# A phase's two pairs of attention scores in four neighbouring banks, with one exponential of 2048 columns

## The chip, the cores and the metric

The kernel runs on one core of a Trainium2 chip. The metric is the time of one execution in microseconds (us) of device time. All times below are in us unless they are marked ns. The engines go by the profile's names: PE is TensorE (its weight loads are PEld), ACT is ScalarE, DVE is VectorE, POOL is GpSimd and SP is SyncE, which issues the DMAs.

## The reference

The input x has 2048 tokens of 512 channels, in float32. Two branches are mixed by a gate of each token:

```python
g = sigmoid((x * gate_w).sum(-1, keepdims=True))
a = attention(x, wqkv, wo)       # 32 heads of 16, softmax over all 2048 keys
b = token_mlp(x, w1, b1, w2, b2) # layernorm, then gelu MLP 2048 -> 1792 -> 2048 over tokens
return g * a + (1 - g) * b

def attention(x, wqkv, wo):
    q, k, v = ...                # (1, 32, 2048, 16) each, from x @ wqkv
    scores = q @ k.T * 16 ** -0.5
    p = softmax(scores, axis=-1)
    return (p @ v).reshape(B, S, 512) @ wo
```

The attention has 32 heads of 2048 x 2048 scores, each of which goes through one exponential.

## The kernel before, in words

The first stages make v, the stacks of q and k, the layernorm and the first layer of the MLP. They fill about the first 278 us. The rest is the attention, and beside it PE does the second layer of the MLP, the late queries and the first half of the output projection.

**Phases.** The attention is a loop of 128 phases (L992). A group `grp` is a pair of heads over half of the queries; it has four phases (`PHASES`, `ph`), and there are 32 groups. A phase makes 16 tiles of scores, called units `n` = 0 to 15, each of 128 keys by 512 queries in one PSUM bank (matmul L1065). A matmul of scores uses 64 of PE's rows. For the first `n_b` units another matmul, from the list `beside`, runs in the other 64 rows (L1074). `n_b` is 14 in phases with a step of the second layer (16 tiles, three steps each, two phases a step) and 12 in phases with a late query or a projection. The order of the units is `in_turn`: 0 to 13, then 14 and 15, or 0 to 13, then 15 and 14.

**Who takes a score out of its bank.** Units in `SINGLE` (0, 2, 4, 6, 7, 8) go through one exponential of 512 columns on ACT (L1091). Units in `EVAC` (1, 3, 5, 9, 14, 15) are copied by DVE to SBUF (L1087), and one exponential of 3072 columns works on all six there (L1100). Units 10 and 11, and 12 and 13 (`TWO`), lie in two neighbouring banks each, as one tile `t`, and each pair goes through one exponential of 1024 columns (`exps`, L1029).

**Banks.** Seven of eight banks serve scores, the eighth (`dn`) the matmuls beside. `shares(n)` gives the order in which a phase uses the seven: unit n < 7 goes to bank `share[n]`, unit 7 to 9 to `share[n - 7]`. Then a second set of tiles is laid over the same banks: units 10 to 13 go to `share[3]` to `share[6]`, unit 14 to `share[0]`, unit 15 to `share[2]`, and `av`, in which the products with v add up, to `share[1]`. Both sets come from pools that are opened with `reuse_waits="tile"` (`regions`). The argument of `shares` is the bank that the phase before gives back last (`spare`).

**Products with v.** After its scores a phase multiplies exponentials with v (`apply_v`, L961, 64 matmuls a phase): first the three `HELD` pairs of the phase before, then this phase's five `TURNS`, of which (10, 11) and (12, 13) come last. DVE then adds `av` to the group's sum (L983). In a group's first phase the held pairs close the group before in `av`, and the new group starts in another bank, `twos[spare]`.

**The order is written out.** Inside `tc.manual_schedule` every engine works in the order of the program. `call(p, ...)` puts an action ahead of phase p's scores, DMAs on SP's queue above all; `on_dve(p, ...)` puts a step on DVE behind the copies of phase p, ahead of the additions from `av`; `amid` puts one between the copies. `fetch` issues the DMAs of a block of attention outputs and leaves three steps on DVE for later phases (`ats`): the product with the inverse sums, a rounded copy, and the rest. `fetch_right` and `fetch_o` fetch such blocks; `load_wq` brings rows of the last weights, with two steps on DVE; `end_constants` makes four small constants. In this late stage `p0` is 112.

Of the kernel before, what the change touches and what calls it, by code (L numbers as in the profile page):

```python
# [9 lines left out]
F32 = mybir.dt.float32  # L10
# [3 lines left out]
AF = mybir.ActivationFunctionType  # L14
ALU = mybir.AluOpType
AX = mybir.AxisListType
SYNC = mybir.DependencyInfo(mybir.DependencyClass.Sync, mybir.DependencyReason.DATA)
AHEAD_OF_USE = "the next group's scores find their stacks awaited"
REASON = "the two halves of the rows add to one bank"
EARLY = "a later instruction of this engine then waits for one engine alone"  # L20
# [3 lines left out]
P = 128  # L24
# [8 lines left out]
NB = 512  # L33
NQ = S // NB
VC = DH + 1
SCALE = DH**-0.5
# [24 lines left out]
def gated_mix(ctx: ExitStack, tc: tile.TileContext, a_x, a_wqkv, a_wo, b_w1, b_b1, b_w2, b_b2, gate_w, out):  # L61
    nc = tc.nc
# [115 lines left out]
    with tc.tile_pool(name="vp", bufs=1, side="right") as pool:  # L178
# [143 lines left out]
        y, t, w = (pool.tile([P, NS], F32, name=n) for n in "ytw")  # L322
# [103 lines left out]
    with tc.tile_pool(name="gl", bufs=2, side="right") as gl:  # L426
# [74 lines left out]
        for f0, cs in order.items():  # L501
            n = min(NB, F - f0) // P
# [32 lines left out]
    ptp = att_ctx.enter_context(tc.tile_pool(name="pt", bufs=2, reuse_waits="tile"))  # L535
# [10 lines left out]
    for i, p in reversed(list(enumerate(ps))):  # L546
        u = out_pool.tile([P, D], F32, name="row", bufs=3)
        at = NF - len(ps) + i
# [32 lines left out]
    PHASES, NSC, BANKS = 4, 16, 7  # L581
# [20 lines left out]
    wq, between = [], {}  # L602
# [84 lines left out]
    def call(at, *what):  # L687
        calls.setdefault(at, []).append(what)

    def on_dve(at, *what):  # L690
        later.setdefault(at, []).append(what)
# [42 lines left out]
    def load_wq(at):  # L734
        wq.extend(v_block(0)[:, 8 * n : 8 * n + 8].rearrange("p (i t) x -> p i t x", i=2) for n in range(2))
        raw = end.tile([P, QW], F32, name="o_sum", bufs=3).rearrange("p (i c) -> p i c", i=2)
        nc.gpsimd.memset(raw, 0.0)
        for j in range(4):
            nc.sync.dma_start(
                raw[32 * j : 32 * j + DH], a_wo[(H - 2) * DH : H * DH, :].rearrange("(i r) c -> r i c", i=2)  # L740
            )
        raw = raw.rearrange("p i (t x) -> p i t x", x=P)
        on_dve(at + 2, nc.vector.tensor_copy, wq[0], raw)
        on_dve(at + 3, nc.vector.tensor_tensor, wq[1], raw, wq[0].bitcast(F32), ALU.subtract)

    def invert(half, k, pairs, at):

# [128 lines left out]
    at, queries = 0, [(b, n) for n in (2, 3) for b in range(ND)]  # L876
    for t in range(NS):
        at = put(second_layer(t), at, [14] * 3)
        if queries:
            b, n = queries.pop(0)  # L880
            at = put_whole(late_query(b, n), at)
# [9 lines left out]
    for half in range(2):  # L891
        for k in range(ND):
            pairs = 3 if half and k == ND - 1 else 4
            p0 = PHASES * (half * NP + 4 * k + pairs) + 1
            call(p0, invert, half, k, pairs, p0 + (2, 2, 1, 0)[k] if half else p0 + 2)
    left, right = slice(0, NB), slice(NB, QW)
    for k in range(ND):
        p0 = PHASES * (NP + 4 * (k // 2 + 1)) + 3 + 4 * (k % 2)
        assert p0 + 3 < 2 * at
        call(p0, fetch_left, k, p0 + 2, p0 + 3, p0 + 3)  # L900
    p0 = 2 * at
    call(p0, open_end)
    on_dve(p0 + 13, end_constants)
    for k in range(ND):
        call(p0 + k, fetch_right, k, p0 + k + 2, p0 + k + 2, p0 + k + 2)
    for t in range(NH):
        at = put_whole(project(t), at)
        call(p0 + 2 * t, load_base, NH + t)
    assert p0 + 7 < 2 * (at - 4) and at == NG * PHASES // 2
    call(p0 + 4, fetch_o, 0, p0 + 6, p0 + 6, p0 + 7)  # L910
    call(p0 + 6, fetch_o, 1, p0 + 8, p0 + 8, p0 + 10)
    call(p0 + 7, load_wq, p0 + 7)
    call(p0 + 9, fetch_o, 2, p0 + 11, p0 + 12, p0 + 12)
    call(LAST, lambda: fetch_o(3, LAST, LAST, LAST, pairs=3))

    token, mark = (out_pool.tile([1, 1], F32, name=name, bufs=1) for name in ("token", "mark"))
# [3 lines left out]
    TWO = (10, 11), (12, 13)  # L920
    TURNS = [(0, 2), (4, 6), (7, 8), *TWO]
    HELD = [(1, 3), (5, 9), (14, 15)]

    def shares(n):

        for one in range(0, BANKS, 2):
            lows = [k for k in range(one)][::2] + [k for k in range(one + 1, BANKS)][::2]
            for third in lows:
                if n in (third, third + 1):
                    first, second = (low for low in lows if low != third)  # L930
                    return [first, first + 1, one, second, second + 1, 2 * third + 1 - n, n]


    def regions():
# [53 lines left out]
    with tc.manual_schedule(engines=engines):  # L988
# [3 lines left out]
        for p in range(LAST + 1):  # L992
            grp, ph = divmod(p, PHASES)
            second = ph % 2
# [28 lines left out]
                    turn = 1 - turn  # L1023

            def exps(n):
                pt = ptp.tile([P, 2, NB], F32, name="p2", bufs=len(TWO))
                where = [share[(j - BANKS) % BANKS] for j in (n - 1, n)]
                low = min(where)
                pairs_done.append(nc.scalar.activation(pt, twos[low, low + 1], AF.Exp, scale=SCALE))  # L1029
                for j, k in zip((n - 1, n), where):  # L1030
                    units[j] = *units[j][:3], pt[:, k - low, :]

            pairs_done = []
# [6 lines left out]
            for n in in_turn:  # L1040
                i, qb = head[n], qbs[n]
                c = at[i][qb]
                at[i][qb] += 1
                if n < TWO[0][0]:
                    if n >= BANKS:
                        ones[share[n - BANKS]] = psum.tile([P, NB], F32, name=f"s{share[n - BANKS]}")
                    s = ones[share[n % BANKS]]
                else:
                    if n == TWO[0][0]:
                        pool.__exit__(None, None, None)  # L1050
                        pool = regions()
                        psum = pool.__enter__()
                        twos = {}
                        for low in range(BANKS):
                            if low == share[1]:
                                av = psum.tile([P, NB], F32, name="av")
                            elif low in (share[0], share[2]):
                                twos[low] = psum.tile([P, NB], F32, name=f"u{low}")
                            elif low not in twos:
                                two = psum.tile([P, 2, NB], F32, name=f"t{low}")  # L1060
                                twos[low], twos[low + 1] = two[:, 0, :], two[:, 1, :]
                                twos[low, low + 1] = two
                    s = twos[share[2 if n == NSC - 1 else (n - BANKS) % BANKS]]
                rows_i = slice(i * HALF, i * HALF + ROWS)
                nc.tensor.matmul(  # L1065
                    s,
                    kt[grp][rows_i, c * P : (c + 1) * P],
                    qt[grp][rows_i, qb * NB : (qb + 1) * NB],
                    start=True,
                    stop=True,  # L1070
                )
                if n < n_b:
                    ps, a, b, begin, last, done = beside[n]
                    mm = nc.tensor.matmul(ps, a[half], b[half], start=begin and not second, stop=last and bool(second))  # L1074
                    if n == 0 and fence is not None:
                        tc.add_manual_dep(mm.ins, fence.ins.name, SYNC, reason=REASON)
                    if n == n_b - 1:
                        fence = nc.gpsimd.memset(token, 0.0)  # L1078
                        tc.add_manual_dep(fence.ins, mm.ins.name, SYNC, reason=REASON)
                if n == in_turn[-2]:  # L1080
                    if n_b and second and beside[-1][-1] in between:
                        between[beside[-1][-1]]()
                    for what, *args in amid.get(p, ()):
                        what(*args)
                if n in EVAC:
                    pt = evac[:, EVAC.index(n), :]
                    nc.vector.tensor_copy(pt, s)  # L1087
                    units[n] = i, c, qb, pt
                elif n in SINGLE:
                    pt = ptp.tile([P, NB], F32, name="p1", bufs=len(SINGLE))  # L1090
                    one = nc.scalar.activation(pt, s, AF.Exp, scale=SCALE)  # L1091
                    if n == SINGLE[-1] and p:
                        tc.add_manual_dep(one.ins, earlier.ins.name, SYNC, reason=EARLY)
                    units[n] = i, c, qb, pt
                else:
                    units[n] = i, c, qb, None
                    if n in (TWO[0][1], TWO[1][1]):
                        exps(n)
            for x in ([evac] if p < LAST else [evac[:, :2, :], evac[:, 2:, :]]):
                done = nc.scalar.activation(x, x, AF.Exp, scale=SCALE)  # L1100
            tc.add_manual_dep(done.ins, pairs_done[0].ins.name, SYNC, reason=EARLY)
            evac_done.append(done)
            earlier = pairs_done[1]
            if n_b and second and beside[-1][-1]:
                beside[-1][-1]()
            if p == 0:
# [14 lines left out]
            if ph == 0:  # L1121
                if held:
                    apply_v(av, grp - 1, held, final=True)
                    spare = share[3]
                    av = twos[spare]
                apply_v(av, grp, turns)
            elif p < LAST:
                apply_v(av, grp, held + turns, await_loads=ph == PHASES - 1)
            else:
                ot = sums[grp]  # L1130
                nc.vector.tensor_scalar_max(ot, ot, least[0])
                apply_v(av, grp, held + turns + now_held, final=True)
                last_ot = ot
# [170 lines left out]
```

## Time and profile before

| | us |
|---|---|
| median of 3 runs | 1266.68 |
| lowest and highest | 1266.62, 1266.8 |
| the profiled execution's own time | 1266.69 |
| its span in the profile | 1264.9 |
| granted clock of TensorE, mean | 0.999 |

The page shares the span out by engine, follows back the chain of work that ended last, and groups instructions by line, engine and tiles: a row has the count, the summed busy time, the mean length of one in ns, and the idle time before them with what ended it. The timeline lists instructions in order of time: start, length, engine, line, operation, tiles, shape and count, where neighbours that are alike are put together; in brackets stands idle time of the engine just before, with what ended it. A start on ACT may lie before the end of the instruction ahead of it, so lengths there overlap.

### The profile page before, as it was taken

To read this page: it belongs to the slowest core of one execution; us is meant where nothing else is said; L and a number is where in the kernel's file an instruction comes from. 1 tells how busy PE (TensorE), PEld (TensorE's weight loads), DVE (VectorE), ACT (ScalarE), POOL (GpSimd) and SP (SyncE) were. 2 spreads that over 40 slices of the span, in tenths; PEclk is the share of its full clock that TensorE was granted. 3 is DMA by queue.
4 is the path that set the end of the run, shared out by engine and by line. 5 is a ranking of instruction groups with operands and counts; after the bars stand their busy time and mean duration, and the time that the engine had idled before them with its cause. 6 is when DMAs were issued, how large, how long until landed. Compare 5 with 4: busy or idle time off the path is not lost.

```text
span 1264.9 us, 32830 instructions
## 1 busy us (share of the span) xinstructions
PE 1255.3 (99%) x13342; PEld 828.8 (66%) x13342; DVE 857.4 (68%) x1562; ACT 1069.2 (85%) x1405; POOL 198.9 (16%) x316
## 2 busy tenths in 40 slices
PE   9999999999999999999999999999999999999997
PEld 7888888875666666666666666666666666666656
DVE  5675453178767676767677677777777677678883
ACT  4443343269999999999999999999999999999980
POOL 0220444461010101010110101111111111100000
PEclk9999999999999999999999999999999999999999
DMA  4799443244744544634344433444553443366611
GB/s 134 255 327 339 140 123 105 80 128 114 210 123 102 92 99 83 160 83 97 84 101 95 106 85 79 93 90 80 113 101 81 80 99 60 56 166 185 143 58 70
DMA packets 100556, 152.32 MB, mean 120 GB/s; under 512 B 17109, under 2 KB 56171, under 8 KB 96300
## 3 DMA queue, kind: packets, MB, share of 16 engines
q1 hardware_dynamic: 99820, 149.08, 46.3%
q8 instruction: 107, 1.75, 0.6%
q10 hardware_dynamic: 576, 1.05, 0.2%
q14 instruction: 53, 0.43, 0.1%
HBM read 105.39 MB, written 44.68 MB: 119 GB/s over the span
## 4 chain that ended last, share of the span: by engine, by line
PE 95%; DVE 2%; ACT 2%; DMA 0%; issue 0%; SPq 0%; DVEq 0%; ACTq 0%
PE av L961 30%; PE s L1065 20%; PE acc L424 12%; PE acc L75 8%; PE t L1065 8%; PE t L961 5%; PE dn L1074 4%; PE u L1065 3%; PE pa L1156 2%; DVE pe L1087 2%; ACT pe L1100 1%; ACT p L1091 1%; PE acc L199 1%; PE acc L268 1%; ACT p L1029 0%; DVE ot L983 0%
## 5 line engine op out<-in xcount | busy, mean ns | idle before, releaser
L1091 ACT ACTIVATE p<-s 128x512 f32<-128x512 f32 x768 | 412.2, 786 | 0.1
L1100 ACT ACTIVATE pe<-pe 128x3072 f32<-128x3072 f32 x129 | 380.6, 2952 | 0.6 <-DVE pe L1087 0.6
L1065 PE MATMUL s<-qs,ks 64*128 64x512 f32 x1280 | 330.6, 400 | 0.8 <-ACT p L1091 0.6
L1087 DVE COPY pe<-s 128x512 f32<-128x512 f32 x512 | 323.9, 686 | 5.5 <-PE s L1065 1.7
L1065 PEld LDWEIGHTS s<-qs,ks 64*128 64x128 f32 x1280 | 225.6, 184 | 94.3 <-issue 52.3
L1029 ACT ACTIVATE p<-t 128x1024 f32<-128x1024 f32 x256 | 277.6, 1259 | 0.0
L961 PE MATMUL av<-p,v 128*32 128x256 f32 x3880 | 227.2, 379 | 0.0
L1087 DVE COPY pe<-u 128x512 f32<-128x512 f32 x256 | 165.0, 686 | 66.8 <-PE u L1065 66.8
L961 PE MATMUL av<-pe,v 128*32 128x256 f32 x3072 | 192.5, 383 | 0.4 <-ACT pe L1100 0.4
L983 DVE TENSOR_TENSOR ot<-av,ot 128x512 f32<-128x512 f32 (+2 forms) x160 | 93.2, 583 | 143.9 <-PE av L961 142.5
L68 POOL TENSOR_TENSOR w_lo<-w_raw,w_hi 128x512 fp32r<-128x512 f32 (+1 forms) x128 | 153.1, 1203 | 197.0 <-ACT w_hi L67 99.8
L1074 PE MATMUL dn<-u_hi,w_lo 64*128 64x512 f32 x448 | 180.8, 403 | 0.0
L961 PEld LDWEIGHTS av<-p,v 128*32 128x32 f32 x3880 | 126.0, 110 | 83.3 <-ACT p L1091 0.2
L1074 PE MATMUL dn<-u_lo,w_hi 64*128 64x512 f32 x448 | 180.6, 403 | 0.0
L1074 PE MATMUL dn<-u_hi,w_hi 64*128 64x512 f32 x448 | 180.5, 403 | 0.0
L1065 PE MATMUL t<-qs,ks 64*128 64x512 f32 x512 | 142.2, 412 | 0.0
L961 PEld LDWEIGHTS av<-pe,v 128*32 128x32 f32 x3072 | 86.8, 109 | 81.1 <-ACT p L1091 35.6
L1078 POOL MEMSET token<- 1x1 f32 x128 | 11.4, 89 | 747.4 <-PE dn L1074 657.3
L67 ACT CAST w_hi<-w_raw 128x512 fp32r<-128x512 f32 (+1 forms) x67 | 38.0, 569 | 82.5 <-PE acc L424 63.1
L1065 PEld LDWEIGHTS t<-qs,ks 64*128 64x128 f32 x512 | 73.1, 184 | 50.9 <-ACT p L1091 48.8
L424 PE MATMUL acc<-h_hi,w_hi 128*128 128x512 f32 x224 | 87.9, 392 | 0.0
L424 PE MATMUL acc<-h_hi,w_lo 128*128 128x512 f32 x224 | 87.8, 392 | 0.0
(162 smaller groups left out, 1615.0 us busy)
## 6 DMA issues: line engine op xcount, KB each, us to landing
w_raw<-in_B_w_dram SPq DMA_DIRECT2D x96, 256.0 KB
ks<-kp SPq DMA_DIRECT2D x192, 128.0 KB
qs<-qp SPq DMA_DIRECT2D x256, 64.0 KB
kp<-pc SPq DMA_DIRECT2D x16, 512.0 KB
qp<-pc SPq DMA_DIRECT2D x8, 768.0 KB
qp<-row SPq DMA_DIRECT2D x24, 256.0 KB
v<-v SPq DMA_DIRECT2D x4, 1088.0 KB
x<-in_A_x_dram SPq DMA_DIRECT2D x16, 256.0 KB
```

What stands on the lines that cost most here:

```text
L67: copy(hi, src)
L68: return sub(lo, src, hi.bitcast(F32), ALU.subtract)
L75: nc.tensor.matmul(ps, a, b, start=start and n == 0, stop=stop and n == last)
L424: nc.tensor.matmul(p, a, b, start=first and k == 0, stop=last and k == 2)
L961: mm = nc.tensor.matmul(av[32 * j : 32 * (j + 1), i * QC : (i + 1) * QC], vb[b][:, v_at : v_at + 32], pt[:, h * QC : (h + 1) * QC], start= ...
L983: latest["add"] = nc.vector.tensor_tensor(x, y, x, ALU.add)
L1029: pairs_done.append(nc.scalar.activation(pt, twos[low, low + 1], AF.Exp, scale=SCALE))
L1065: nc.tensor.matmul(s, kt[grp][rows_i, c * P : (c + 1) * P], qt[grp][rows_i, qb * NB : (qb + 1) * NB], start=True, stop=True,)
L1074: mm = nc.tensor.matmul(ps, a[half], b[half], start=begin and not second, stop=last and bool(second))
L1087: nc.vector.tensor_copy(pt, s)
L1091: one = nc.scalar.activation(pt, s, AF.Exp, scale=SCALE)
L1100: done = nc.scalar.activation(x, x, AF.Exp, scale=SCALE)
```

## The change

Units 10 to 13 get one tile of four neighbouring banks (`FOUR`), and `exps` runs once a phase, behind unit 13, on 2048 columns, into one buffer of four blocks of 512 in place of two buffers of two blocks. `shares` is rewritten so that `share[3]` to `share[6]` are four neighbours. In a group's first phase the new sum goes to `share[0]` in place of `share[3]`. Two orderings inside ACT refer to other instructions. Some late steps on DVE move to other phases. Which units go by DVE, the order of units, and the products with v stay.

```diff
-        on_dve(at + 2, nc.vector.tensor_copy, wq[0], raw)
-        on_dve(at + 3, nc.vector.tensor_tensor, wq[1], raw, wq[0].bitcast(F32), ALU.subtract)
+        on_dve(at + 4, nc.vector.tensor_copy, wq[0], raw)
+        on_dve(at + 6, nc.vector.tensor_tensor, wq[1], raw, wq[0].bitcast(F32), ALU.subtract)
...
-    on_dve(p0 + 13, end_constants)
+    on_dve(p0 + 7, end_constants)
     for k in range(ND):
-        call(p0 + k, fetch_right, k, p0 + k + 2, p0 + k + 2, p0 + k + 2)
+        call(p0 + k, fetch_right, k, *(p0 + n for n in ((2, 2, 2), (3, 3, 3), (4, 4, 5), (5, 6, 6))[k]))
...
-    call(p0 + 4, fetch_o, 0, p0 + 6, p0 + 6, p0 + 7)
-    call(p0 + 6, fetch_o, 1, p0 + 8, p0 + 8, p0 + 10)
+    call(p0 + 4, fetch_o, 0, p0 + 6, p0 + 7, p0 + 8)
+    call(p0 + 6, fetch_o, 1, p0 + 9, p0 + 10, p0 + 10)
     call(p0 + 7, load_wq, p0 + 7)
-    call(p0 + 9, fetch_o, 2, p0 + 11, p0 + 12, p0 + 12)
+    call(p0 + 9, fetch_o, 2, p0 + 12, p0 + 14, p0 + 14)
...
+    FOUR = range(10, 14)
+
     def shares(n):
 
-        for one in range(0, BANKS, 2):
-            lows = [k for k in range(one)][::2] + [k for k in range(one + 1, BANKS)][::2]
-            for third in lows:
-                if n in (third, third + 1):
-                    first, second = (low for low in lows if low != third)
-                    return [first, first + 1, one, second, second + 1, 2 * third + 1 - n, n]
+        one = 6 if n < 6 else 0
+        lows = [low for low in range(BANKS) if low % 2 == (one == 0) and low != one]
+        at = next(k for k, low in enumerate(lows) if n in (low, low + 1))
+        third, second = lows[at], lows[1 if at != 1 else 0]
+        first = next(low for low in lows if low not in (second, third))
+        return [first, first + 1, one, second, second + 1, 2 * third + 1 - n, n]
...
             def exps(n):
-                pt = ptp.tile([P, 2, NB], F32, name="p2", bufs=len(TWO))
-                where = [share[(j - BANKS) % BANKS] for j in (n - 1, n)]
+                pt = ptp.tile([P, len(FOUR), NB], F32, name="p4", bufs=1)
+                where = [share[j - BANKS] for j in FOUR]
                 low = min(where)
-                pairs_done.append(nc.scalar.activation(pt, twos[low, low + 1], AF.Exp, scale=SCALE))
-                for j, k in zip((n - 1, n), where):
+                pairs_done.append(nc.scalar.activation(pt, twos["four"], AF.Exp, scale=SCALE))
+                for j, k in zip(FOUR, where):
                     units[j] = *units[j][:3], pt[:, k - low, :]
...
                             elif low not in twos:
-                                two = psum.tile([P, 2, NB], F32, name=f"t{low}")
-                                twos[low], twos[low + 1] = two[:, 0, :], two[:, 1, :]
-                                twos[low, low + 1] = two
+                                four = twos["four"] = psum.tile([P, len(FOUR), NB], F32, name=f"t{low}")
+                                for k in range(len(FOUR)):
+                                    twos[low + k] = four[:, k, :]
...
-                    if n in (TWO[0][1], TWO[1][1]):
+                    if n == FOUR[-1]:
                         exps(n)
...
-            tc.add_manual_dep(done.ins, pairs_done[0].ins.name, SYNC, reason=EARLY)
+            tc.add_manual_dep(done.ins, one.ins.name, SYNC, reason=EARLY)
             evac_done.append(done)
-            earlier = pairs_done[1]
+            earlier = pairs_done[0]
...
-                    spare = share[3]
+                    spare = share[0]
                     av = twos[spare]
```

## The prediction

> **What bounds the kernel now.** I read the page first, then the timeline of two attention phases engine by engine, then the waits of the score tiles. The page:
>
> ```profile
> span 1264.9 us, 32830 instructions
> PE 1255.3 (99%) x13342; PEld 828.8 (66%) x13342; DVE 857.4 (68%) x1562; ACT 1069.2 (85%) x1405; POOL 198.9 (16%) x316
> PE 95%; DVE 2%; ACT 2%; DMA 0%; issue 0%; SPq 0%; DVEq 0%; ACTq 0%
> L1091 ACT ACTIVATE p<-s 128x512 f32<-128x512 f32 x768 | 412.2, 786 | 0.1
> L1100 ACT ACTIVATE pe<-pe 128x3072 f32<-128x3072 f32 x129 | 380.6, 2952 | 0.6 <-DVE pe L1087 0.6
> L1029 ACT ACTIVATE p<-t 128x1024 f32<-128x1024 f32 x256 | 277.6, 1259 | 0.0
> ```
>
> The chain names PE, but the three exponential groups show ACT idle for under 1 us in 128 phases. Both look full, and a busy PE is modelled, so I look at one phase on ACT:
>
> ```profile
> 709.30 3.23 ACT L1091 ACTIVATE p<-s 128x512 f32<-128x512 f32 x6
> 712.18 2.19 ACT L1029 ACTIVATE p<-t 128x1024 f32<-128x1024 f32 x2
> 714.01 3.00 ACT L1100 ACTIVATE pe<-pe 128x3072 f32<-128x3072 f32 x1
> 716.71 3.24 ACT L1091 ACTIVATE p<-s 128x512 f32<-128x512 f32 x6
> 724.13 1.28 ACT L1091 ACTIVATE p<-s 128x512 f32<-128x512 f32 x2
> ...
> 865.34 3.02 ACT L1091 ACTIVATE p<-s 128x512 f32<-128x512 f32 x6
> ```
>
> A phase lasts 7.42 (716.71 to 724.13). Starts overlap the instruction before, so I go by ends. The singles end at 712.53, the two pairs at 714.37, the big one at 717.01, the next singles at 719.95: 1.84 for two pairs, 2.64 for 3072 columns, 2.94 for six singles. So in a full queue a single costs 0.49, a pair 0.92, and the sum 2.94+1.84+2.64 = 7.42 is the whole period: ACT sets the pace here, and PE follows it with small waits. The last row is a batch that met an idle ACT: 3.02 = 0.57 + 5 x 0.49, so an instruction that finds the queue empty takes about 0.09 more.
>
> Now what PE waits for in that phase, and its starts:
>
> ```profile
> 710.27 1.28 ACT L1091 ACTIVATE p<-s 128x512 f32<-128x512 f32 x2
> ...
> 711.12 0.18 PEld L1065 LDWEIGHTS t<-qs,ks 64*128 64x128 f32 x1 [0.19 <-ACT p L1091]
> 711.23 0.19 PEld L1065 LDWEIGHTS t<-qs,ks 64*128 64x128 f32 x1
> 711.60 0.18 PEld L1065 LDWEIGHTS t<-qs,ks 64*128 64x128 f32 x1 [0.19 <-ACT p L1091]
> 712.58 0.16 PEld L961 LDWEIGHTS av<-pe,v 128*32 128x32 f32 x8 [0.26 <-ACT p L1091]
> ...
> 708.76 0.50 PE L1065 MATMUL s<-qs,ks 64*128 64x512 f32 x1
> 710.97 0.39 PE L1065 MATMUL s<-qs,ks 64*128 64x512 f32 x1
> 711.20 0.41 PE L1065 MATMUL t<-qs,ks 64*128 64x512 f32 x1
> 712.18 0.46 PE L1065 MATMUL u<-qs,ks 64*128 64x512 f32 x2
> 712.59 0.42 PE L961 MATMUL av<-pe,v 128*32 128x256 f32 x4
> 716.18 0.50 PE L1065 MATMUL s<-qs,ks 64*128 64x512 f32 x1
> ...
> L1065 PEld LDWEIGHTS t<-qs,ks x446: 182/183/189, 400.1 to 1224.8; 64*128 64x128 f32 x149
>   ACT p L1091: 42.0, 207
> ```
>
> I call the scores by their number n in the code. The first row is the singles of scores 4 and 6; they end at 711.55. Score 12 loads its weights at 711.60, just behind. Score 10 loads at 711.12, one single earlier, behind that of score 4. But score 10's own bank, share[3], held score 3, which DVE copied; score 4 sat in share[4], the other bank of the same two-bank tile. So the first matmul into a tile waits until **all** its banks are free; 11 and 13 wait for nothing. 207 waits among 446 loads of t, four a phase, say that this is so in nearly every phase: two in four.
>
> **The change, part by part.** *One exponential for two.* From 0.49 to 0.92 is 0.43 for 512 columns, so the fixed part in a full queue is 0.06, and 2048 columns cost 0.92 + 2 x 0.43 = 1.78 against 1.84. If ACT went on setting the pace that is -0.06 x 128 = -7.7. The Trainium skill, ScalarE: Activation LUTs, section What ACT_TABLE_LOAD costs, gives an ACTIVATE 186 ns plus 0.833 a column, 93 more for a pointer operand, and an overlap of 93 back to back; an estimate from it is 0.09 to 0.19 saved, 12 to 24 in all. The rows give less, and I keep 0.06.
>
> *One tile of four banks.* share[3] to share[6] held scores 3, 4, 5 and 6. So score 10 now waits for the single of score 6 and the copy of score 5; before, it waited for score 4's. That is one single, 0.49, later, on PE with all of 10 to 15 and the av products queued behind it. And the exponential starts when score 13 is written, where the first pair started behind 11 and was covered. This wait isn't in the trace of before, so I cost the two loops that now close through score 10, from rows above and these, of the stage where PE does stand still:
>
> ```profile
> 1178.67 0.68 DVE L1087 COPY pe<-s 128x512 f32<-128x512 f32 x1
> 1179.47 0.18 PEld L1065 LDWEIGHTS t<-qs,ks 64*128 64x128 f32 x1 [0.28 <-issue]
> 1179.50 0.46 PE L1065 MATMUL t<-qs,ks 64*128 64x512 f32 x1
> 1179.81 0.39 PE L1065 MATMUL t<-qs,ks 64*128 64x512 f32 x1
> 1180.10 0.49 PE L1065 MATMUL t<-qs,ks 64*128 64x512 f32 x2
> 1180.60 0.50 PE L1065 MATMUL u<-qs,ks 64*128 64x512 f32 x2
> 1181.04 0.84 PE L961 MATMUL av<-pe,v 128*32 128x256 f32 x10
> ...
> 710.75 0.68 DVE L1087 COPY pe<-s 128x512 f32<-128x512 f32 x1
> 712.63 1.29 DVE L1087 COPY pe<-u 128x512 f32<-128x512 f32 x2 [0.54 <-PE u L1065]
> ```
>
> ACT's loop: end of score 6's single; 0.05 to the load, 0.03 to the matmul (1179.47 to 1179.50); 0.31 to score 11, for after a stand the second start is late (1179.50 to 1179.81); 0.23 each to 12 and 13 (710.97 to 711.20); 0.39 for the matmul and 0.04 to ACT (708.76 + 0.50 to 709.30); the exponential on an empty queue 1.78 + 0.09 = 1.87; the big one 2.64; four singles 1.96. Sum 7.75.
>
> PE's loop with DVE: first score to the end of the third copy, that of score 5, 711.43 - 708.76 = 2.67; 0.12 to the load (copy of score 3 ends 1179.35, load of score 10 at 1179.47); 0.03; 0.31; three times 0.23 to 12, 13 and the u pair; 0.41 to av (712.18 to 712.59); 3.59 for the av products to the next first score (712.59 to 716.18). Sum 7.82. The larger sets the period: +0.40.
>
> That holds for phases with 14 matmuls beside the scores: 16 tiles of the second layer, three steps each, two phases a step, 96. In the other 32 phases, with 12 beside, 12 and 13 start together, and so do 14 and 15 (the x2 rows), so a slot goes: 2.67 + 0.12 + 0.03 + 0.31 + 0.23 + 0.23 + 0.44 + 3.59 = 7.62, +0.20. Before, the u pair came 0.50 behind 12 here, but 12 had itself waited for a copy; I take 0.23, and 0.50 as the upper end (+0.27 x 32 = 9).
>
> *What hides the rest.* The copies of 14 and 15 end 0.23 + 0.45 + 1.29 = 1.97 after score 13 starts, the exponential of four 0.43 + 1.87 = 2.30 after: the big exponential stays behind ACT, by 0.3; if DVE is later than that, it counts in full. The av products of 10 to 13 come last of 64, after some 0.64 + 0.75 x 3.59 = 3.3, so they find the four ready, 1.0 early. On a group's first phase the new sum goes into share[0], the bank of score 14, free after its copy (1.4 after 13), where the held products last to about 2.0. The order kept between ACT's own instructions costs nothing: both are long done.
>
> *DVE's late steps.* Their number and length stay. Those of right blocks 2 and 3, of the second half's blocks 0 to 2 and of wq go a phase or more later, end_constants goes six earlier. The fetches that issue their DMAs on SP stay where they were, so SP's order is the same; only the buffers are given back later, which POOL's clearing for wq also waits for. The trace shows what is at stake:
>
> ```profile
> 1174.39 1.22 DVE L1117 TENSOR_TENSOR o_sum<-e,o_sum 128x1024 f32<-128x1024 f32 x1
> 1175.65 0.69 DVE L1117 CAST e<-o_sum 128x1024 fp32r<-128x1024 f32 x1
> 1177.24 3.25 ACT L1091 ACTIVATE p<-s 128x512 f32<-128x512 f32 x6
> 1185.19 2.04 ACT L1091 ACTIVATE p<-s 128x512 f32<-128x512 f32 x4
> ```
>
> With 1.91 of steps ahead of a group's closing additions the next phase takes 7.95. The new spread leaves about 1.2 there. At three or four such phases it can give back 0.5 each, 1 to 2 in all; I take -1.
>
> **Sum.** The profiled execution took 1266.69, its span 1264.9 and 1.8 around it, equal to the median 1266.68. 96 x 0.40 = 38.4, 32 x 0.20 = 6.4, less 1: 1266.7 + 43.8, about **1311**. If the late second start (0.31) shrinks to 0.23, both loops lose 0.08: 1301. If the exponential costs up to two pairs on an empty queue, 1.96, ACT's loop is 7.84 and little changes; with the 0.50 above, 1320. So the case itself runs from 1301 to 1322.
>
> **Rivals.** *The wait is by bank (faster).* The Trainium skill, PSUM — Partial Sum Buffer, section PSUM bank collisions raise a hardware error, says what must be guarded is a bank with its quadrant, no more. If score 10 waited for its own bank alone, it would start as now, score 13 would be written at 711.20 + 3 x 0.23 + 0.39 = 712.28, ACT comes free of the singles at 712.53, nothing stands, and 0.06 a phase is saved: 1259. It decides on one fact, whether score 10's load follows the single of 6. The load at 711.12 following its neighbour's single speaks against it, and all 207 waits do. 10 in 100.
>
> *DVE becomes the bound (slower still).* The third copy already ends 2.67 after the first score, and the loop through it is the larger. If additions or steps make it late in one phase of four as at 1177.24 (7.95 for 7.42, about 0.5), 32 x 0.5 = 16 more: 1327. For it: no slack is left on that loop. Against: steps sit behind the copies, and that gap is as long as before. 12 in 100.
>
> *PE catches up.* If the stand on PE were filled, so that only ACT's loop with no late start and no fill counts (7.75 - 0.08 - 0.09 = 7.58), 96 x 0.16 gives 15, and with the short phases near no change about 1282. Nothing is queued on PE that could overtake score 10. 4 in 100.
>
> **Numbers.** Forecast 74, DVE 12, bank 10, PE 4. The range takes the forecast's own and most of the DVE case: 1298 to 1328; the faster case stays outside. About 0.2%, 2.5 us, is what a measurement can tell from no change: faster 0.10, within 0.01, slower 0.89.
>
> **What would show it.** Right: score 10's load stands for about half a microsecond, behind ACT's single or DVE's copy; the group of 2048 columns counts 128 with a mean near 1.9 to 2.0 and ACT idle before it, released by PE, some 30 to 55 us in all; phases 7.8 apart, and 7.6 in the last 16; PE's second load of t without a wait. Wrong: t's loads wait as briefly as now and the phases come at 7.36 (by bank), or the idle time stands before the big exponential, ended by DVE's copies.

## The result, and the profile after

The changed kernel takes 1303.74 us (median; 1303.48 to 1304.12), the kernel before 1266.66 beside it. The ratio is 1.0293, with a 95% interval of 1.0279 to 1.0306: slower by 37.1. The profiled execution took 1304.12, 1302.2 of it the span, at a clock of 0.999. The page of the changed kernel:

```profile
span 1302.2 us, 32562 instructions
PE 1261.6 (97%) x13342; PEld 838.0 (64%) x13342; DVE 857.8 (66%) x1562; ACT 1074.0 (82%) x1277; POOL 198.8 (15%) x316
ACT 60%; PE 36%; issue 3%; DVE 1%; DVEq 0%
...
L1093 ACT ACTIVATE p<-s 128x512 f32<-128x512 f32 x768 | 387.8, 616 | 0.5 <-PE s L1067 0.5
L1102 ACT ACTIVATE pe<-pe 128x3072 f32<-128x3072 f32 x129 | 353.3, 2740 | 0.0
...
L1031 ACT ACTIVATE p<-t 128x2048 f32<-128x2048 f32 x128 | 240.5, 1879 | 33.5 <-PE dn L1076 25.3
...
L1067 PE MATMUL t<-qs,ks 64*128 64x512 f32 x512 | 145.6, 418 | 32.2 <-ACT p L1093 30.1
```

ACT has 128 instructions fewer and became the chain's first engine, although it is idle more: 33.5 before the exponential of 2048 columns, 0.26 a phase, where the pairs had 0.0. PE stands 32.2 before its matmuls of t, released by ACT's singles. Two engines that wait for each other form a loop: each waits for the other once a phase, and the way round the loop is longer than either engine's own work. The waits of t's weight loads say which score stands:

```profile
L1067 PEld LDWEIGHTS t<-qs,ks x512: 182/185/187, 280.8 to 1262.9; 64*128 64x128 f32 x171
its engine sat idle before it (us, times) until:
  ACT p L1093: 86.6, 128
```

There are 128 waits among 512 loads. Before, the whole run had 239 waits behind ACT among 512 loads, at scores 10 and 12 (the 207 among 446 are those from 400 us on). Now each of the 128 phases has one: score 10 waits, for 0.68, and 11, 12 and 13 do not. One phase in the timeline, ACT first, then weight loads, then PE and DVE (lines of matmuls beside the scores left out):

```profile
588.08 3.03 ACT L1093 ACTIVATE p<-s 128x512 f32<-128x512 f32 x6
591.40 1.88 ACT L1031 ACTIVATE p<-t 128x2048 f32<-128x2048 f32 x1 [0.30 <-PE dn L1076]
593.18 2.76 ACT L1102 ACTIVATE pe<-pe 128x3072 f32<-128x3072 f32 x1
595.83 1.56 ACT L1093 ACTIVATE p<-s 128x512 f32<-128x512 f32 x3
...
590.17 0.18 PEld L1067 LDWEIGHTS t<-qs,ks 64*128 64x128 f32 x1 [0.68 <-ACT p L1093]
...
590.17 0.49 PE L1067 MATMUL t<-qs,ks 64*128 64x512 f32 x1 [0.26 <-ACT p L1093]
590.51 0.39 PE L1067 MATMUL t<-qs,ks 64*128 64x512 f32 x1
590.74 0.39 PE L1067 MATMUL t<-qs,ks 64*128 64x512 f32 x1
590.97 0.39 PE L1067 MATMUL t<-qs,ks 64*128 64x512 f32 x1
591.21 0.39 PE L1067 MATMUL u<-qs,ks 64*128 64x512 f32 x2
591.52 1.05 PE L963 MATMUL av<-pe,v 128*32 128x256 f32 x13
...
588.13 2.52 DVE L1089 COPY pe<-s 128x512 f32<-128x512 f32 x4
```

The six singles end at 591.11, so the fourth, that of score 6, ended two times 0.49 earlier, at 590.13. Score 10 loads 0.04 to 0.05 later. DVE's copy of score 5, the third of the four in the last row, ended at about 590.04 (an estimate from the length of that row), only some 0.1 earlier. Scores 11 to 13 follow at 0.34, 0.23 and 0.23; the exponential of four starts 0.43 behind the start of score 13 and ends at 593.28 (1.88), the big one at 595.94 (2.66), and four singles of the next phase (0.49 each) close the loop: 0.05 + 0.80 + 0.43 + 1.88 + 2.66 + 1.95 = 7.77. ACT stands from 591.11 to 591.40, until score 13 is written; the row names `dn`, the matmul that runs beside score 13. The median phase with 14 matmuls beside, from first score to first score, is 7.765 (7.418 before).

### The profile page after: what moved, and what is told of

Read it like the earlier page. It is cut to its first block, busy times and chain, and to the rows that moved or that the text cites. A ratio compares the mean times of both kernels' runs of the same rounds, so it can differ in the third digit from the quotient of the medians.

```text
span 1302.2 us, 32562 instructions
## 1 busy us (share of the span) xinstructions
PE 1261.6 (97%) x13342; PEld 838.0 (64%) x13342; DVE 857.8 (66%) x1562; ACT 1074.0 (82%) x1277; POOL 198.8 (15%) x316
## 3 DMA queue, kind: packets, MB, share of 16 engines
q10 hardware_dynamic: 576, 1.05, 0.2%
## 4 chain that ended last, share of the span: by engine, by line
ACT 60%; PE 36%; issue 3%; DVE 1%; DVEq 0%
ACT pe L1102 26%; ACT p L1093 18%; ACT p L1031 15%; PE acc L424 12%; PE t L1067 10%; PE acc L75 8%; PE pa L1158 2%; PE dn L1076 1%; DVE pe L1089 1%; PE u L963 1%; PE acc L199 1%; PE av L963 1%; PE acc L268 0%; PE acc L245 0%; DVE ot L985 0%
## 5 line engine op out<-in xcount | busy, mean ns | idle before, releaser
L1093 ACT ACTIVATE p<-s 128x512 f32<-128x512 f32 x768 | 387.8, 616 | 0.5 <-PE s L1067 0.5
L1102 ACT ACTIVATE pe<-pe 128x3072 f32<-128x3072 f32 x129 | 353.3, 2740 | 0.0
L1031 ACT ACTIVATE p<-t 128x2048 f32<-128x2048 f32 x128 | 240.5, 1879 | 33.5 <-PE dn L1076 25.3
L1067 PE MATMUL t<-qs,ks 64*128 64x512 f32 x512 | 145.6, 418 | 32.2 <-ACT p L1093 30.1
L1067 PEld LDWEIGHTS t<-qs,ks 64*128 64x128 f32 x512 | 79.4, 185 | 94.8 <-ACT p L1093 86.6
```

Source lines behind the costliest of these rows:

```text
L1031: pairs_done.append(nc.scalar.activation(pt, twos["four"], AF.Exp, scale=SCALE))
L1067: nc.tensor.matmul(s, kt[grp][rows_i, c * P : (c + 1) * P], qt[grp][rows_i, qb * NB : (qb + 1) * NB], start=True, stop=True,)
```

## The experiments

**Is the cost the tile's wait or the late exponential?** `two_exps` keeps the four-bank tile and its wait and goes back to two exponentials, so that ACT can start on scores 10 and 11 before 13 is written. The last line of the edit voids a wait of scores 12 and 13 for the first exponential, which reads the other half of the tile.

```diff
-                pt = ptp.tile([P, len(FOUR), NB], F32, name="p4", bufs=1)
+                pt = ptp.tile([P, 2, NB], F32, name="p2", bufs=len(TWO))
...
-                pairs_done.append(nc.scalar.activation(pt, twos["four"], AF.Exp, scale=SCALE))
+                pairs_done.append(nc.scalar.activation(pt, half_of, AF.Exp, scale=SCALE))
...
+                if n in TWO[1]:
+                    tc.declare_no_dep(score.ins, pairs_done[0].ins, reason="the tile's other two banks")
```

> The change's tile of four banks with its wait, but two exponentials of 1024 columns on its halves, the first behind score 11 as before the change. Theory A: score 10 still waits for the single of 6 and the copy of 5, at 2.8 after the first score. ACT's loop falls to about 7.39, but PE's (2.80 + 0.35 + 3 x 0.23 + 0.33 + 3.59) stays at 7.76, so 1299 to 1304, nearly nothing comes back. Rival B (the late start of the exponential): ACT is fed from score 11 on, phases return to 7.42, total 1266 to 1270. If only ACT's loop was real and PE's was mis-sized: between, 1275 to 1295.

It took 1301.25 (1300.63 to 1301.56), ratio 1.0273 (1.0259 to 1.0286). That is 34.4 above the 1266.81 beside it, so Theory A holds: nearly all of the 37.1 stays without the late exponential. Its page, then a phase of it, PE first and DVE's copies last:

```profile
L1105 ACT ACTIVATE pe<-pe 128x3072 f32<-128x3072 f32 x129 | 354.5, 2749 | 12.7 <-DVE big L67 0.4
...
L1032 ACT ACTIVATE p<-t 128x1024 f32<-128x1024 f32 x256 | 248.8, 1027 | 0.9 <-PE dn L1079 0.9
L1068 PE MATMUL t<-qs,ks 64*128 64x512 f32 x512 | 142.0, 409 | 30.7 <-DVE pe L1092 27.1
```

```profile
601.32 0.50 PE L1068 MATMUL s<-qs,ks 64*128 64x512 f32 x1
...
604.13 0.46 PE L1068 MATMUL t<-qs,ks 64*128 64x512 f32 x1 [0.24 <-DVE pe L1092]
604.43 0.39 PE L1068 MATMUL t<-qs,ks 64*128 64x512 f32 x1
604.66 0.39 PE L1068 MATMUL t<-qs,ks 64*128 64x512 f32 x1
604.90 0.39 PE L1068 MATMUL t<-qs,ks 64*128 64x512 f32 x1
605.12 0.42 PE L1068 MATMUL u<-qs,ks 64*128 64x512 f32 x2
605.48 1.50 PE L963 MATMUL av<-pe,v 128*32 128x256 f32 x24
606.80 2.34 PE L963 MATMUL av<-p,v 128*32 128x256 f32 x40
609.07 0.50 PE L1068 MATMUL s<-qs,ks 64*128 64x512 f32 x1
...
602.09 2.52 DVE L1092 COPY pe<-s 128x512 f32<-128x512 f32 x4
```

ACT now has slack (12.7 before the big one), and PE's stand before t ends at DVE's copies, where the changed kernel showed ACT's singles. (The weight loads still name ACT, 82.1 in 128 waits. But by the rows the single of score 6 ended at about 603.93 and the copy of score 5 at about 604.00; the load at 604.10 comes 0.1 behind the copy, the distance that the prediction read as 0.12.) What is left is the loop of PE with DVE alone: from 601.32 to 609.07, 7.75, median 7.744. So both loops of the prediction exist, at 7.765 and 7.744, and taking one away gains only the 0.02 a phase down to the other.

**Would score 10's own bank be enough?** `by_bank` makes the four-bank tile at the start of the phase, and takes out by hand the waits of a score for readers of the tile's other banks.

```diff
+                if k == low:
+                    four = twos["four"] = psum.tile([P, len(FOUR), NB], F32, name=f"t{low}")
+                if k in share[3:]:
+                    twos[k] = four[:, k - low, :]
...
+                    for other, reader in readers.items():
+                        if other != bank and other in share[3:]:
+                            tc.declare_no_dep(score.ins, reader.ins, reason="another bank of the tile")
```

> One exponential of 2048 columns as in the change, but the tile of four banks is taken at the start of the phase and serves scores 3 to 6 and 10 to 13, and a score's wait for readers of the tile's other banks is declared void. So score 10 waits for its own bank alone (the copy of score 3). The first writer of the tile is now score 3, which waits for DVE's addition from the old av bank, some 0.16 us on PE. Theory A (the wait for all four banks closes the loops through score 10): score 10 starts 2.4 to 2.6 after a phase's first score instead of 2.8, phases of 7.36 to 7.42, total 1259 to 1268. Rival B (the cost is that the exponential stands behind score 13, wherever 10 starts, or that one instruction over four banks is itself slow): ACT goes on standing 0.2 to 0.3 a phase, total 1295 to 1304.

It took 1444.35 (1444.15 to 1444.82), ratio 1.1401 (1.1386 to 1.1416), outside both expectations and 141 above the change. The waits by engine, as us in total, times and longest:

```profile
ACT p L1092 <- DVE pe L1086: 106.5, 132, 0.8
...
DVE pe L1086 <- ACT p L1092: 91.6, 126, 1.0
```

Scores 3 to 6 now sit in one tile, two read by DVE and two by ACT, and the program made these readers wait for one another in turn, though they read different banks. PE then waited for both. So the edit had moved the tile's wait to another place, and did not test what it was made for. `by_bank_free` takes those out as well:

```diff
+                    if n < BANKS and bank in share[3:]:
+                        for other in (m for m in readers if m % 2 != n % 2):
+                            tc.declare_no_dep(read.ins, readers[other].ins, reason="another bank of the tile")
+                        readers[n] = read
```

> As by_bank, and the readers of the tile's banks (DVE's copies of 3 and 5, ACT's singles of 4 and 6) no longer wait for one another; that wait was what took by_bank to phases of 8.84. Score 10 waits for the copy of 3, 11 for the single of 4, 12 for the copy of 5, 13 for the single of 6; still one exponential of 2048 columns. Theory A (the wait for all four banks is the cost): score 10 starts at 2.4 to 2.65, ACT has no idle time before the 2048 columns, ACT needs 7.36 a phase, PE 7.40 to 7.44 where score 3 stands for the old av bank: total 1261 to 1269. Rival B (one instruction over four banks behind score 13 is the cost): 1290 to 1304.

It took 1280.2 (1279.83 to 1280.72), ratio 1.0107 (1.0092 to 1.0122), between the two expectations. Score 10 was released (no wait of its load is left), and 23.5 of the 37.1 are back. The loads of t show what is not:

```profile
L1060 PEld LDWEIGHTS t<-qs,ks x1024: 182/184/189, 279.0 to 1239.3; 64*128 64x128 f32 x171
its engine sat idle before it (us, times) until:
  DVE ot L985: 33.8, 96
```

```profile
594.59 0.18 PEld L1060 LDWEIGHTS s<-qs,ks 64*128 64x128 f32 x1 [0.41 <-issue]
...
595.47 0.18 PEld L1060 LDWEIGHTS t<-qs,ks 64*128 64x128 f32 x1 [0.35 <-DVE ot L985]
...
594.73 0.69 DVE L985 TENSOR_TENSOR ot<-s,ot 128x512 f32<-128x512 f32 x1 [1.89 <-PE s L963]
```

Score 3, now the tile's first writer, waits for DVE's addition out of `av`'s old bank (ends 595.42, load 595.47), in 96 phases. That bank is score 6's, `share[6]`; score 3 has no need of it. Phases are 7.57, but 7.38 where the addition before them is done in parts of 256 columns and ends sooner.

**Is one exponential worth anything here?** `by_bank_pairs` is `by_bank_free` with two exponentials, by the edit of `two_exps`, and without the waits of these two for DVE's copies out of the tile.

> As by_bank_free, but two exponentials of 1024 columns on the halves of the tile. Beside by_bank_free it shows what one instruction in place of two is worth when neither waits. Theory A: ACT needs 7.42 a phase, 0.06 more: 1266 to 1270, 0 to 7 above by_bank_free, the more the more often ACT and not PE sets the pace. If the rule of a fixed 0.09 to 0.19 a piece held: 8 to 24 above, where ACT sets the pace.

It took 1280.09 (1279.89 to 1280.78), ratio 1.0109 (1.0094 to 1.0124): no difference. While PE's stand at score 3 sets the pace, a fixed cost saved on ACT is worth nothing.

**Score 3's wait.** `add_by_bank` was to let score 6 alone wait for the addition; `add_by_bank_pairs` is the same with two exponentials.

```diff
+                if p and n in (3, 4, 5):
+                    for add in latest["adds"]:
+                        tc.declare_no_dep(score.ins, add.ins, reason="another bank of the tile")
+                if p and n == BANKS - 1:
+                    for add in latest["adds"]:
+                        tc.add_manual_dep(score.ins, add.ins.name, SYNC, reason=REASON)
```

> The kernel with one four-bank tile for the whole phase and waits bank by bank (1280.2), with one more wait put where it belongs: DVE's addition from the bank that the phase before gave back last is now awaited by score 6, which writes that bank, and no longer by scores 3, 4 and 5, which write the tile's other banks. Nothing is left out. Theory A (score 3's wait is what is left of the loss): three phases of four, at 7.57 before, come to the 7.38 of the fourth; 0.19 x about 84 = 16 us, so 1261 to 1266, below the 1266.6 of the kernel without the change. Rival B (the 7.57 comes from something else, say the load behind the last u at 3.98, with 0.47 between them, or from ACT): phases stay at 7.5 or more, and the time between 1274 and 1281.

> The same with two exponentials of 1024 columns in place of one of 2048. Theory A (with all waits by bank ACT is again close to the bound, and the fixed part of an instruction, 0.06, counts): phases of 7.42 in place of 7.36 to 7.39, so 3 to 7 us above its sibling with one exponential, about 1266 to 1268. Rival B (PE sets the pace at 7.38, whatever ACT does): the two within 1 us of each other. If score 3's wait was not the cause, both stay near 1280.

They took 1280.25 (ratio 1.0109, 1.0092 to 1.0125) and 1280.47 (1.0111, 1.0094 to 1.0128). That reads like rival B, but the edit did not do what it says: the wait is still there.

```profile
594.86 0.18 PEld L1062 LDWEIGHTS t<-qs,ks 64*128 64x128 f32 x1 [0.35 <-DVE ot L986]
```

It seems that a new tile laid over old ones begins with a wait for whatever the old ones still have open, which declaring the pair free does not touch. So the two runs say nothing about theory A. `whole_tile` makes one tile of all seven banks, once, for the whole attention, so that nothing is ever laid over anything, and takes out every wait between different banks by name; a bank's own waits stay, and so do all waits through SBUF.

```diff
+        whole = psum.tile([P, BANKS, NB], F32, name="t")
...
+    def touch(inst, on, who, pt=None):
+        for before, banks, engine in hist:
+            if engine == who or banks & on or before is maker.get(id(pt)):
+                continue
+            if who == "PE" or engine != "PE":
+                tc.declare_no_dep(inst.ins, before.ins, reason="another bank of the tile")
+        hist.append((inst, on, who))
...
-                    s = twos[share[2 if n == NSC - 1 else (n - BANKS) % BANKS]]
...
+                s, on = whole[:, bank, :], {bank}
```

> All seven banks of the scores are one tile that lasts for the whole attention, and every wait between two of its banks is taken out by hand, the one on DVE's addition from the bank given back last among them; each bank keeps its own waits, and one exponential of 2048 columns stays. Nothing is left out. It carries out what add_by_bank meant to (there score 3 went on waiting, because a tile that is laid over others begins with a wait for all of them). Theory A (score 3's wait for the addition is what is left of the loss): its load comes at 0.62 in place of 0.88, phases at 7.38 and below, 1258 to 1265, under the 1266.6 of the kernel without the change. Rival B (PE's stand only moves, to score 6, whose bank the addition frees, or to the products with v): phases of 7.5 and more, 1274 to 1281.

> The same with two exponentials of 1024 columns in place of one of 2048. Theory A (with all waits by bank ACT is close to the bound again, and the fixed part of an instruction, 0.06, counts): phases of 7.42 in place of 7.36 to 7.38, 3 to 8 us above its sibling, 1265 to 1268, as the kernel without the change. Rival B (PE sets the pace whatever ACT does): the two within 1 us of each other.

`whole_tile` took 1264.27 (1263.84 to 1265.16), ratio 0.998 (0.9971 to 0.9989): 0.2% faster than the kernel before and 39 us faster than the change. `whole_tile_pairs` took 1267.13 (1266.59 to 1267.66), ratio 1.0002 (0.9993 to 1.0011). Theory A holds for both in the main (the difference is just under the 3 to 8 expected): all 37 us of the change were waits for banks that the waiting score does not touch, and with them gone one exponential for two is worth 1267.13 - 1264.27 = 2.86, where the prediction's terms gave 7.7. (Both hold the new steps on DVE, worth about 1 below, so "all" is meant to some 1 us.) Why not 7.7, the exponentials of a phase of each show, `whole_tile` first, its chain ahead of them, and behind them PE's first score, its score 13 and the first score of the next phase:

```profile
PE 89%; DVE 9%; ACT 1%; issue 1%; DVEq 0%
...
580.34 2.76 ACT L1110 ACTIVATE pe<-pe 128x3072 f32<-128x3072 f32 x1
582.99 3.03 ACT L1098 ACTIVATE p<-t 128x512 f32<-128x512 f32 x6
585.95 1.88 ACT L1050 ACTIVATE p<-t 128x2048 f32<-128x2048 f32 x1
587.73 2.76 ACT L1110 ACTIVATE pe<-pe 128x3072 f32<-128x3072 f32 x1
...
582.41 0.50 PE L1070 MATMUL t<-qs,ks 64*128 64x512 f32 x1
...
585.53 0.39 PE L1070 MATMUL t<-qs,ks 64*128 64x512 f32 x1
...
589.80 0.50 PE L1070 MATMUL t<-qs,ks 64*128 64x512 f32 x1
```

```profile
581.31 3.00 ACT L1110 ACTIVATE pe<-pe 128x3072 f32<-128x3072 f32 x1
584.01 3.24 ACT L1098 ACTIVATE p<-t 128x512 f32<-128x512 f32 x6
586.89 2.20 ACT L1050 ACTIVATE p<-t 128x1024 f32<-128x1024 f32 x2
588.72 3.01 ACT L1110 ACTIVATE pe<-pe 128x3072 f32<-128x3072 f32 x1
```

With pairs the ends are 584.31, 587.25, 589.09 and 591.73: 2.94 + 1.84 + 2.64 = 7.42, ACT's full queue as before the change. With one they are 583.10, 586.02, 587.83 and 590.49: 2.92 + 1.81 + 2.66 = 7.39. The last matmul, score 13, starts at 585.53 and is written some 0.43 later, at 585.96, just as ACT comes free: the exponential finds a queue that is all but empty, as the 1.88 of it says. In this phase PE's matmuls follow one another without a stand and take 7.39 by themselves (582.41 to 589.80), and the chain of the run lies on PE and DVE, ACT with 1%. So PE's own work now sets the pace, at 7.39. ACT's full queue would take 7.36 with one exponential and 7.42 with two, so only half of the 0.06 could show.

**The late steps on DVE.** `old_steps` is the changed kernel with the steps where they were; `new_steps` is the kernel before with the steps spread as in the change.

```diff
-    call(p0 + 4, fetch_o, 0, p0 + 6, p0 + 7, p0 + 8)
+    call(p0 + 4, fetch_o, 0, p0 + 6, p0 + 6, p0 + 7)
...
-    call(p0 + 9, fetch_o, 2, p0 + 12, p0 + 14, p0 + 14)
+    call(p0 + 9, fetch_o, 2, p0 + 11, p0 + 12, p0 + 12)
```

> The change with DVE's late steps where they were before it. Theory A: the three phases that open a group late (117, 121, 125) have their copies late by up to 0.6 as before the change and pay 0.2 to 0.6 each: 1304.5 to 1306. Rival D (the new spread itself costs, because steps now stand in phases that had none): 1300 to 1303.

> The kernel before with DVE's late steps spread as in the change. Theory A: the phases of 7.88 to 7.97 in the last stage fall to about 7.65, 0.2 to 0.3 each: 1265.5 to 1266.3. Rival D (the new spread costs): 1267 to 1269.

`old_steps` took 1304.58 (1304.12 to 1304.98), ratio 1.0297 (1.0284 to 1.0311), 0.84 above the change (0.7 when each is set against the kernel before beside it). `new_steps` took 1265.76, ratio 0.9992 (0.9983 to 1.0), 1.05 below the 1266.81 beside it: at the edge of what can be told, and the same 1 us from the other side. Three late phases of the kernel before took 7.88 to 7.97 from first score to first score; of `new_steps` 7.65 to 7.66, as here:

```profile
1176.77 3.14 ACT L1091 ACTIVATE p<-s 128x512 f32<-128x512 f32 x6
1184.42 3.01 ACT L1091 ACTIVATE p<-s 128x512 f32<-128x512 f32 x6
```

## Why the prediction was right, point by point

**Score 10 waits for the last of four banks: right.** 128 waits of 0.68 (about half a microsecond was forecast), all behind ACT's singles, none for 11 to 13.

**ACT's loop, 7.75: right**, 7.765 measured. Its terms measured: 0.34 for 0.31 to score 11, 0.43 for 0.39 + 0.04, 1.88 for 1.87, 2.66 for 2.64.

**PE's loop with DVE, 7.82, taken as the larger: wrong in size and so in rank.** `two_exps` shows it alone, at 7.744. The term that was mis-sized is the 0.41 from the u pair to `av`: in the phase it was read from, the first `av` load, at 712.58, came 0.05 behind the end of ACT's singles at 712.53, the same distance as any release by ACT, and its row names ACT in brackets, so the 0.41 held a wait. In `two_exps` it is 0.36 (605.12 to 605.48), with the 3.59 behind it as predicted (605.48 to 609.07). The hundredths of the other terms make the rest. So ACT's loop binds, and a phase costs 0.347 more and not 0.40: 96 x 0.05 = 5 of the 7.3 by which 1311 was too high.

**Short phases, +0.20: too much.** With one slot of 0.23 gone, ACT's loop is 7.52, and the timeline has

```profile
1199.34 3.03 ACT L1093 ACTIVATE p<-s 128x512 f32<-128x512 f32 x6
1206.87 3.03 ACT L1093 ACTIVATE p<-s 128x512 f32<-128x512 f32 x6
```

7.53 for the predicted 7.62, which came from PE's loop; `two_exps` has 7.52 for it there, so it too was sized too large. The first sixteen such phases cost about 1.8, the late stage, steps included, about 2.0, together 3.8 against 6.4 - 1. With 96 x 0.347 = 33.3 that is 37.1, as measured. So the mechanism was right and two terms were sized too large. Both errors lie on the same side, so the hit does not rest on errors that cancel.

**The late steps, -1: right** (0.84 and 1.05, both at the edge of what can be told).

**What hides the rest: right.** The big exponential never waits (0.0), and the products with v hardly do for the four (0.3 in the whole run).

**The rivals.** *By bank* was right that the chip needs no more than a wait by bank, and wrong that the program would do so; its 1259 was 5 too low, since PE's own work takes 7.39. The Trainium skill, PSUM — Partial Sum Buffer, section PSUM bank collisions raise a hardware error, asks for a guard by bank and quadrant; `whole_tile`, guarded by bank alone, agrees with it (1264.27). *DVE becomes the bound* did not come: the late phases with steps are 7.79 at most. *PE catches up* did not come either: nothing fills the stand of 32.2.

## What to carry to other kernels

To merge instructions, one merges the buffers that they read, and with a merged buffer the first writer waits for the last of all earlier readers: cost the wait on the loop that it closes before counting the fixed cost saved (here 37 us against 3). A loop's terms must be read from rows that hold no wait of their own, or the wrong loop is taken as the bound. An edit that removes a wait is looked up in the trace before its time is read: twice here the wait had only moved or stayed.

## What was not expected of the hardware

A matmul that starts after a stand is followed by the next at 0.30 to 0.34 and not 0.23 (590.17 to 590.51; 604.13 to 604.43), so a stand costs about 0.1 more than its own length. The prediction had this from one row (0.31), and it held. A stand is not the only occasion: the first score behind the products with v is followed at 0.34 too (582.41 to 582.75 in `whole_tile`), and its row shows no idle time on PE before it. Why the second matmul is late stays open. The Trainium skill, ScalarE: Activation LUTs, section What ACT_TABLE_LOAD costs, gives 186 ns and 0.833 ns a column; the estimate from it for 2048 columns is 1.89, and the 1.88 of an exponential on an empty queue agrees. In a full queue the rows leave about 0.06 of fixed cost for an instruction saved (0.49, 0.92 and 2.64 for 512, 1024 and 3072 columns), less than the 0.09 to 0.19 that the prediction estimated from this section of the Trainium skill. The time shows less still, 2.86 in 128 phases or 0.022 each, since PE sets the pace there.
